# A gated mix of a state-space convolution and a feed-forward network: the block-wise convolution replaced by one 2048-point transform in two TensorE stages

## The chip, the cores and the metric

The kernel runs on one core of a Trainium2 chip. The metric is the time of one execution on the device, in microseconds (us). Times of a kernel are medians of its runs. The five engines named below are TensorE (PE in the profile; PEld is its weight load), VectorE (DVE), ScalarE (ACT), GpSimd (POOL) and SyncE (SP), which here issues nearly all DMA transfers.

A run of one core can be a per cent or two slower than the fastest run of the same kernel. Such runs are marked slow. They are left out of all ratios, but not of the medians quoted; where that matters, the fast runs are given too. (One run of the kernel before took 634.8 us; it too is marked slow.) Chips differ too: the kernel before took 350.6 to 353.1 us (medians) on most of the chips used and 357.3 to 357.7 us on two others, so kernels are compared by their ratio to the kernel before on the same chip wherever a few per cent matter.

## The reference, cut to what matters

```python
# u: [1, 2048, 640] bf16, 128 states per channel, 1728 hidden features
dt = exp(log_dt)[:, None]
logdA = dt * (A_re + 1j * A_im);  dB = dt * (B_re + 1j * B_im)
P = exp(logdA[:, :, None] * l)                       # l = 0..2047
K = einsum("dn,dnl,dn->dl", C_re + 1j * C_im, P, dB).real
y = irfft(rfft(pad(u)) * rfft(pad(K)))[:2048] + u * Dskip     # causal convolution per channel
b = (gelu(u @ w_gate) * (u @ w_up)) @ w_down
g = sigmoid((u * gate_w).sum(-1))
out = g * y + (1 - g) * b
```

Three pieces of work share the core: generating the kernel K (exponentials, sines and a sum over the 128 states), the convolution, and the feed-forward network (FFN).

## The kernel before

Both kernels put all their work into a list of steps, each with its engine, an estimated duration and a priority. A list scheduler in the Python code then fixes the order of instructions on every engine, before anything is built. The order is therefore part of the program: an engine runs its instructions in that order, and a wait at the head of its queue holds up whatever is behind.

K is not evaluated at all 2048 positions. Exponentials and sines are taken on two small grids of positions, for all channels, and a small matmul per channel, summing over the states, combines the two ("the contraction"). The states lie on the 128 partitions, and along the free dimension there are table entries and channels. In the kernel before, four neighbouring channels lie side by side in these tables:

```python
# before: e1[p, channel group k, 4*entry + channel in group]
def quads(ap):
    return ap.rearrange("p (k j) -> p k j", j=4)

def exps1(p, g):
    ...
    nc.scalar.activation(out=e1[:, :, 4 * r:4 * r + 4], in_=quads(aT[:, ds]), func=ACT.Exp,
                         scale=float(sg * (4 + 8 * i)))              # line 420, 128x320
def exps2(p, g):
    ...
    nc.scalar.activation(out=e2[p][:, :, 4 * e:4 * e + 4], in_=quads(aT[:, ds]), func=ACT.Exp,
                         scale=float(X2[e] + CENTRE))                # line 430, 128x320
def sins(k, ph, n, w, dst, keys):                                    # line 466, up to 128x2560
    nc.scalar.activation(out=dst, in_=ph.bitcast(I16)[:, :, :, 0:8 * n:2], func=ACT.Sin, scale=SIN_SCALE)
```

The convolution cuts the 2048 tokens into four blocks. Each block of u and of K is transformed by matmuls with a cosine and sine table, the spectra of all pairs of blocks that matter are multiplied and summed on VectorE (`product`, line 904), and a second set of matmuls transforms back. The inputs are transposed by DMA at the start.

```python
# before: one product of block spectra; n pairs of blocks at once, then selected and summed
def tm(out, a, b, op):
    nc.vector.tensor_tensor(out=out, in0=a, in1=b, op=op)            # line 904
...
ve(..., lambda: tm(x, u[:, ::1 - 2 * q, rev, ds], kb[:, :, 0:n, ds], ALU.mult), ...)
```

## Time and profile before

| | before |
|---|---|
| time, median of 3 runs | 351.87 us (351.23 to 353.12) |
| PE busy | 299.7 us, 84% of the span |
| DVE busy | 297.8 us, 84% |
| ACT busy | 237.2 us, 67% |
| bytes moved by DMA | 25.46 MB |

The head of the profile page of the kernel before: busy time of each engine, then the span in 40 equal slices (8.9 us each), where a digit is the busy share of a slice in tenths. The last row shown is the share of busy time of the 16 DMA engines.

```profile
span 355.9 us, 5682 instructions
...
PE 299.7 (84%) x2182; PEld 175.8 (49%) x2182; DVE 297.8 (84%) x528; ACT 237.2 (67%) x374; POOL 15.7 (4%) x32
...
PE   0048459999999999999785679999999999999885
...
DVE  8999899756368898999893806999999999998962
ACT  6999699999999899999964779999111011100000
...
DMA  6684632003100201102552710052400005003321
```

There are three stages. Until about 43 us PE has little to do. From 60 to 200 us PE and ACT are both nearly full. From 216 us on DVE and PE are full, and from about 250 us ACT is nearly idle. The windows view of the kernel before gives that in numbers (columns: window, its length, then busy time and instructions of PE, PEld, DVE, ACT, POOL, granted clock, DMA share, GB/s):

```profile
60.00:200.00 140.00, 129.56 (x970) 64.83 (x969) 109.76 (x213) 126.78 (x202) 9.00 (x9) 0.99 0.24 66
...
216.00:343.00 127.00, 123.92 (x943) 88.50 (x943) 124.97 (x154) 45.22 (x74) 0.00 (x0) 1.00 0.20 48
```

The groups of instructions of the kernel before (columns: line, engine, operation, output and input with partitions x elements, count, total busy us and mean ns of one instruction, idle time before them; nearly all tiles are cut from one buffer, so most operands read `arena`). The page's group of all sizes of the spectrum products:

```profile
L904 DVE TENSOR_TENSOR arena<-arena 128x640 bf16<-128x640 bf16 (+5 forms) x112 | 106.7, 1011 | 1.5 <-ACT arena L998 0.9
```

From the view of the same kernel that keeps sizes apart:

```profile
L904 DVE TENSOR_TENSOR arena<-arena 128x2560 bf16<-128x2560 bf16 x18 | 26.5, 1489 | 1.1 <-ACT arena L998 0.9
...
L420 ACT ACTIVATE arena<-arena 128x320 bf16<-128x320 f32 x64 | 23.3, 465 | 0.0
...
L466 ACT ACTIVATE arena<-arena 128x2560 bf16<-128x2560 int16 x8 | 18.7, 2343 | 0.8 <-DVE arena L459 0.8
...
L430 ACT ACTIVATE arena<-arena 128x320 bf16<-128x320 f32 x42 | 15.5, 459 | 0.0
```

The spectrum products are a third of all VectorE work. An exponential of 128x320 takes 0.46 us and a sine of 128x2560 takes 2.34 us.

### The profile page before, as it was taken

The page shows a single profiled execution, that of the slowest core. Times are in us where ns is not written, and L with a number is a line of the kernel's source. Part 1 is how long each engine was busy: PE and PEld are TensorE (multiplying, and loading weights), DVE is VectorE, ACT ScalarE, POOL GpSimd, SP SyncE. Part 2 cuts the span into 40 slices and gives each one's busy share as a digit, 9 for nine tenths or more (in the row PEclk, how much of TensorE's full clock was granted, in tenths as well). Part 3 has the DMA queues.
Part 4 walks back from the last instruction along what each step waited for, and adds up shares of the span by engine and source line. Part 5 has one row for each costly group of instructions (what it writes and reads, how often), then busy time and mean ns, then how long its engine had stood idle before and what let it go on. Part 6 is the DMA issues. An engine that isn't in the chain of part 4 may idle for free.

```text
span 355.9 us, 5682 instructions
## 1 busy us (share of the span) xinstructions
PE 299.7 (84%) x2182; PEld 175.8 (49%) x2182; DVE 297.8 (84%) x528; ACT 237.2 (67%) x374; POOL 15.7 (4%) x32
## 2 busy tenths in 40 slices
PE   0048459999999999999785679999999999999885
PEld 0012113444555554444343545666777777767664
DVE  8999899756368898999893806999999999998962
ACT  6999699999999899999964779999111011100000
POOL 6000000000000000000071000000000000000000
PEclk9999988999999999999998989999999999999999
DMA  6684632003100201102552710052400005003321
GB/s 111 181 134 98 163 127 88 20 19 76 37 20 19 58 20 37 40 0 55 187 195 61 276 57 0 2 146 61 103 17 0 20 21 91 20 18 49 100 75 57
DMA packets 53019, 25.46 MB, mean 72 GB/s; under 512 B 46400, under 2 KB 50304, under 8 KB 52608
## 3 DMA queue, kind: packets, MB, share of 16 engines
q1 hardware_dynamic: 52608, 23.79, 26.4%
q0 software_dynamic: 384, 1.31, 1.2%
q8 instruction: 17, 0.28, 0.3%
q14 instruction: 10, 0.08, 0.1%
HBM read 12.83 MB, written 6.03 MB: 53 GB/s over the span
## 4 chain that ended last, share of the span: by engine, by line
DVE 38%; PE 27%; ACT 19%; SPq 10%; issue 4%; DMA 1%; another core or an unknown queue 0%; DVEq 0%; ACTq 0%
DVE arena L904 28%; PE ps L588 10%; PE ps L606 8%; SPq L302 7%; ACT arena L466 5%; ACT arena L529 3%; PE ps L524 3%; DVE arena L883 3%; ACT arena L592 3%; PE ps L1015 2%; ACT arena L430 2%; SPq L307 2%; DVE arena L1024 2%; PE ps L846 2%; ACT arena L660 2%
## 5 line engine op out<-in xcount | busy, mean ns | idle before, releaser
L904 DVE TENSOR_TENSOR arena<-arena 128x640 bf16<-128x640 bf16 (+5 forms) x112 | 106.7, 1011 | 1.5 <-ACT arena L998 0.9
L588 PE MATMUL ps<-arena 128*128 128x512 bf16 x280 | 68.5, 396 | 25.9 <-DMA arena<-in_B_w_gate_dram 21.8
L606 PE MATMUL ps<-arena 128*128 128x512 bf16 x260 | 62.3, 382 | 3.2 <-DVE arena L610 3.0
L994 PE MATMUL ps<-arena 128*128 128x320 bf16 x448 | 62.0, 299 | 0.4 <-ACT arena L872 0.4
L588 PEld LDWEIGHTS <-arena 128*128 128x128 bf16 x280 | 27.9, 101 | 61.7 <-DMA arena<-in_B_w_gate_dram 22.2
L998 ACT ACTIVATE arena<-ps,omg 128x640 bf16<-128x640 f32 x16 | 12.7, 794 | 68.3 <-PE ps L994 61.1
L994 PEld LDWEIGHTS <-arena 128*128 128x128 bf16 x448 | 43.6, 98 | 17.2 <-issue 0.6
L610 DVE TENSOR_TENSOR arena<-ps,arena 128x512 bf16<-128x512 f32 x52 | 34.8, 686 | 17.5 <-PE ps L606 13.7
L466 ACT ACTIVATE arena<-arena 128x2240 bf16<-128x2240 int16 (+1 forms) x20 | 43.3, 2184 | 0.9 <-DVE arena L459 0.8
L606 PEld LDWEIGHTS <-arena 128*128 128x128 bf16 x260 | 24.8, 99 | 33.4 <-issue 7.2
L1015 PE MATMUL ps<-arena 128*128 128x320 bf16 x256 | 37.7, 299 | 2.6 <-DVE arena L1024 1.6
L1015 PEld LDWEIGHTS <-arena 128*128 128x128 bf16 x256 | 24.7, 98 | 12.7 <-issue 3.7
L592 ACT ACTIVATE arena<-ps 128x512 bf16<-128x512 f32 (+1 forms) x56 | 28.5, 615 | 0.3 <-PE ps L588 0.2
L529 ACT CAST arena<-ps 128x420 bf16<-128x420 f32 x32 | 20.3, 674 | 10.9 <-PE ps L524 6.9
L420 ACT ACTIVATE arena<-arena 128x320 bf16<-128x320 f32 x64 | 23.3, 465 | 0.0
L456 DVE SCALAR_TENSOR_TENSOR arena<-arena 128x160 int32<-128x160 f32 x84 | 20.8, 319 | 2.3 <-ACT arena L466 2.2
L846 PE MATMUL ps<-arena 128*128 128x320 bf16 x128 | 20.8, 315 | 1.9 <-ACT arena L850 1.6
L872 ACT CAST arena<-ps 128x640 bf16<-128x640 f32 (+1 forms) x40 | 21.1, 618 | 1.4 <-PE ps L866 0.9
L883 DVE TENSOR_TENSOR arena<-arena 128x640 bf16<-128x640 bf16 (+1 forms) x30 | 11.1, 419 | 12.9 <-ACT arena L872 12.9
L866 PE MATMUL ps<-arena 128*128 128x320 bf16 x144 | 21.1, 299 | 0.8 <-ACT arena L872 0.6
L850 ACT ACTIVATE arena<-ps 128x640 bf16<-128x640 f32 x32 | 20.1, 813 | 1.6 <-PE ps L846 1.6
L655 PE MATMUL ps<-arena 128*128 128x512 bf16 x42 | 13.6, 450 | 8.6 <-ACT arena L660 8.1
(92 smaller groups left out, 310.6 us busy)
## 6 DMA issues: line engine op xcount, KB each, us to landing
out_dram<-arena SPq DMA_DIRECT2D x16, 160.0 KB, 1.8
dFK<-arena SPq DMA_DIRECT2D x9, 256.0 KB, 2.0
arena<-in_B_w_gate_dram SPq DMA_DIRECT2D x13, 160.0 KB, 2.9
arena<-in_B_w_up_dram SPq DMA_DIRECT2D x13, 160.0 KB, 2.7
arena<-in_B_w_down_dram SPq DMA_DIRECT2D x13, 160.0 KB, 2.3
arena<-in_A_u_dram SPq DMA_DIRECT2D x4, 320.0 KB, 4.0
dTAB<-arena SPq DMA_DIRECT2D x1, 1024.0 KB, 4.5
arena<-dTAB SPq DMA_DIRECT2D x1, 1024.0 KB, 5.1
```

Of the source, the lines that this page charges most:

```text
L302: dma(1050, lambda: nc.sync.dma_start_transpose(out=xT[tq][:, kt, :], in_=u2[S * tq:S * tq + S, kt * 128:kt * 128 + 128]), w=[("xT", tq, k ...
L420: nc.scalar.activation(out=e1[:, :, 4 * r:4 * r + 4], in_=quads(aT[:, ds]), func=ACT.Exp, scale=float(sg * (4 + 8 * i)))
L466: ac(actns(2 * n * w), lambda: nc.scalar.activation(out=dst, in_=ph.bitcast(I16)[:, :, :, 0:8 * n:2], func=ACT.Sin, scale=SIN_SCALE), r=[( ...
L529: ac(actns(420), lambda k=k, s=s: nc.scalar.copy(out=kst[:, :, 5 * s:5 * s + 5], in_=ps[:, k, 0:420].rearrange("p (g e) -> p e g", e=84)), ...
L588: nc.tensor.matmul(ps[:, k, :], lhsT=Wg[f % 2][:, kt, :], rhs=xT[tq][:, kt, :], start=(kt == 0), stop=(kt == NKT - 1))
L592: ac(actns(512), lambda: nc.scalar.activation(out=HT[f][0:p, tq, :], in_=ps[0:p, k, :], func=ACT.Gelu_apprx_tanh), r=[("bank", k)], w=[("H ...
L606: nc.tensor.matmul(ps[:, 4 + k, :], lhsT=Wu[f % 2][:, kt, :], rhs=xT[tq][:, kt, :], start=(kt == 0), stop=(kt == NKT - 1))
L610: ve(tt(512, 1) + 60, lambda: nc.vector.tensor_tensor(out=HT[f][:, tq, :], in0=ps[:, 4 + k, :], in1=HT[f][:, tq, :], op=ALU.mult), r=[("ba ...
L846: nc.tensor.matmul(ps[:, k + h, 0:DH], lhsT=tab[:, j, q, fsl(ft)], rhs=src[:, j, h * DH:(h + 1) * DH], start=(j == 0), stop=(j == 1))
L904: nc.vector.tensor_tensor(out=out, in0=a, in1=b, op=op)
L994: nc.tensor.matmul(ps[:, k + h, 0:DH], lhsT=HT[f][:, c, 128 * j:128 * j + 128], rhs=Wd[f][:, h * DH:(h + 1) * DH], start=(f == 0), stop=(f ...
L1015: nc.tensor.matmul(ps[:, k + h, 0:DH], lhsT=tab[:, ft, q, 128 * j:128 * j + 128], rhs=U[ft][:, q, c, h * DH:(h + 1) * DH], start=(ft == 0 ...
```

## The change

The intent is to take the 106.7 us of block products off VectorE and the transposes off the start. One transform of 2048 points replaces the block transforms. It is split into two matmul stages, with a transpose between them that is a write to DRAM scratch and a read in another order. The spectra of u and K are multiplied once, and two more stages, with another scratch transpose, bring the product back. K is written to scratch too and gathered from it in the order of tokens. The FFN runs in two groups of 1024 tokens, so that its VectorE and ACT operations have 1024 columns instead of 512. The host hands u and the parameters over already transposed.

The tables of the kernel generation changed layout with it. The new contraction wants, for one channel, all 20 or 32 table entries adjacent in memory. So the channel became the outer index and the table entry the inner one. The core of the diff, with cuts marked by dots:

```diff
-    def exps1(p, g):                      # e1: groups of four channels side by side
+    def exps1(h, i0, n):                  # cs1 = [128, 2, 320 channels, 32 entries]
...
-                    nc.scalar.activation(out=e1[:, :, 4 * r:4 * r + 4], in_=quads(aT[:, ds]), func=ACT.Exp,
-                                         scale=float(sg * (4 + 8 * i)))
+                    nc.scalar.activation(out=cs1[:, 1, :, s], in_=aT[:, ds], func=ACT.Exp, scale=float(sg * (4 + 8 * i)))
...
+        # cs2 = [128, 2, 320 channels, 20 entries]
+                nc.scalar.activation(out=cs2[:, 1, :, e], in_=aT[:, ds], func=ACT.Exp, scale=float(X2[e] + CENTRE))
...
+        # trig = [128, 2, 320 channels, 4 entries]
+        ac(an(2 * n * W), lambda: nc.scalar.activation(out=t[:, :, :, 0:n].rearrange("p q c j -> p q j c"),
+                                                       in_=ph.bitcast(I16)[:, :, 0:n, 0:2 * W:2], func=ACT.Sin, scale=SIN_SCALE),
...
-                            nc.tensor.matmul(ps[:, k, 84 * g:84 * g + 84], lhsT=cs1[c][:, q, k0 + g, :],
-                                             rhs=cs2[c][:, q, k0 + g, :], start=(q == 0), stop=(q == 1))
+                                nc.tensor.matmul(ps[32 * cg:32 * cg + NE, k + b, 32 * i:32 * i + 32], lhsT=cs2[:, q, c, :],
+                                                 rhs=cs1[:, q, c, :], start=(q == 0), stop=(q == 1))
...
+                evac(256 * nb, p, dst.rearrange("p r (b i) -> p b i r", b=nb), ...)      # PSUM -> kst[128, 32, 80]
...
+        # K to scratch in 20 transfers, gathered to token order in 15
+        for e0, n, r0, rs in ((0, 8, 1, 8), (8, 4, 257, 4), (12, 2, 385, 2), (14, 2, 449, 2), (16, 4, 513, 1)):
+            for cg in range(4): ... dma(n * 5, go, r=KK, w=[(f"dS{h}", e0, cg)], rank=0.5)
...
-    def product(c, ft, hs): ...           # 112 tensor_tensor instructions over the pairs of blocks
+    def chain(h, R):
+            ve(v2(2560), lambda c=c, t=t: nc.vector.tensor_tensor(out=U[c][:], in0=U[c][:], in1=t[:], op=ALU.mult), ...)
+            ve(v2(2560), lambda c=c, t=t: nc.vector.tensor_tensor(out=Us[c][:], in0=Us[c][:], in1=t[:], op=ALU.mult), ...)
...
+            dma(640, lambda s=s, g=g: nc.sync.dma_start(out=dKA[h][8 * g:8 * g + 8].rearrange("i q w -> q i w"), in_=ar[s][:]), ...)
```

Everything that concerns K and the convolution is done for two halves of 320 channels, one after the other.

## The prediction

> **What bounds the kernel now.** Three stages, by the busy time in stretches of 20 us. (1) 0 to 43 us: the sync engine issues DMA transposes at 1.26-1.31 us each (chain of waits); matmul starts late and is 13 of 20 us busy even to 60 us. (2) 60-200 us: ACT (18-20 of 20) and PE share the limit; the chain goes through feed-forward matmuls, sines and gelus. (3) 216-343 us: DVE is full (19-20 of 20) while ACT falls to 3 of 20; the chain is 28% line 904, the block-by-block spectrum products, 106.7 us of DVE (groups by line).
>
> **Costs, with durations from the groups and the chain.** Matmuls stream at 216 ns (512 wide) and 136 ns (320 wide).
> - DVE: products become 16 operations of 128x2560 at 1.49 us = 24 us (-83), the spectrum combining (11), selections and folds (11) go. Added: PSUM copies, about 55 x 0.82 = 45; output mixing 32 x 0.55 = 18 (was 14). Up-multiplications of 128x1024 at about 1.22 = 32 (was 35). The kernel-generation work stays near 100; its 10 magnitude multiplications now broadcast along the innermost dimension and should run unpaired, 1.5 us each (Trainium skill, "Vector Engine (DVE) Microarchitecture Reference", section on the perf-mode triggers; no line of this trace shows it). Sum about 260 (was 298).
> - ACT: sines 18 x 2.34 = 42, exponentials 104 x 0.46 = 48, gelus 29, table loads 23 x 1.28 = 30 (unchanged), about 105 copies x 0.74 = 78. Sum about 243 (was 237), spread evenly.
> - PE: feed-forward 117 + down 61 unchanged; transforms 448 x 136 ns = 61 (was about 96 with its Dskip and FK parts); contraction becomes 1280 32-wide matmuls. The logits show 24.7 ns per pair as floor (80 in 1.98 us), also the skill's figure ("TensorE: Matmul & The Clock Gate", part on the issue floor), so 32-40 us (was about 20). Sum about 275.
> - DMA: 25 MB becomes about 60 MB, mostly through DRAM scratch, half in 640-byte pieces. SP transposes vanish.
>
> **By stages, from the emitted order.** Feed-forward starts at about 10 us instead of 60. Up to the first contraction DVE has 97 us and ACT about 90: ends near 103 us. Then to the second contraction PE, ACT, DVE have each about 75-85 us with dependences: ends near 195 us. After it PE has 117 us (52 of transforms, 30 down, 17 up, 17 contraction), DVE 95, ACT 66, and 30 MB of DMA, estimated 110-135 us because the second stage, spectra and transpose back wait for whole scratch writes. The last write-read-transform-store sequence leaves PE partly idle for about 20 us. Total about 320.
>
> **On the critical path:** about 35-45 us of the start-up, and about 80 us of DVE products; given back: PE's larger contraction, scratch round trips and the drained tail. Not all adds up, because the other engines already hold 240-300 us.
>
> **Predicted: 320 us, range 298 to 342.** Faster by over 2%: 0.84; within 2%: 0.10; slower: 0.06.
>
> **What would show each step.** First feed-forward matmul before 12 us. DVE busy 245-275, ACT 230-255, PE mean of contraction matmuls spaced 25-32 ns. DVE's product group about 24 us. DMA packets moved about 60 MB; its share in the last 120 us above half. In the chain, SP/DMA and PE take over from DVE; sync-queue waits on scratch reads of dKA and dY of several us. Idle of the matmul engine concentrated in the last 30 us.
>
> **What would make it wrong.** The 640-byte scratch traffic may be slower than estimated, or many small kernel gathers (about 35 per half, some 0.4 us each to issue) may hold the queue (toward 345). The clock may drop in the contraction or the idle tail. Or downs and stages overlap so well that PE's total bounds it (toward 300).

## The result and the profile after

The changed kernel is correct and takes 516.12 us (515.19 to 517.49, 4 runs) beside 351.55 us of the kernel before on the same chip. The ratio is 1.468, with a 95% interval of 1.464 to 1.473. A ratio here is the mean time of one kernel's fast runs over the mean of the other's fast runs of the same rounds, so it is not quite the ratio of the medians quoted. The change made the kernel 47% slower. The prediction had said 9% faster.

The same head of the page for the changed kernel (slices of 12.9 us):

```profile
span 514.7 us, 6862 instructions
...
PE 301.8 (59%) x2798; PEld 161.3 (31%) x2798; DVE 254.4 (49%) x331; ACT 402.4 (78%) x302; POOL 4.0 (1%) x15
...
PE   0500685993277743934013698664482879988993
...
DVE  7400366774375635232033365443453458757945
ACT  6999999699996999999999959995562556644410
...
DMA  8800011241024222311001142045085799899767
```

VectorE went from 297.8 to 254.4 us, as intended. PE did not change. The DMA moved 60.66 MB. ACT is the surprise: 402.4 us instead of 237.2, and full from the start to about 350 us.

The groups of the changed kernel by size, with the same columns:

```profile
L614 ACT ACTIVATE arena<-arena 128x2560 bf16<-128x2560 int16 x18 | 105.7, 5958 | 0.1
L625 ACT ACTIVATE arena<-arena 128x320 bf16<-128x320 f32 x64 | 89.8, 1885 | 0.9 <-DVE arena L481 0.9
...
L650 ACT ACTIVATE arena<-arena 128x320 bf16<-128x320 f32 x40 | 56.8, 1897 | 0.0
...
L653 DVE TENSOR_TENSOR arena<-arena 128x1280 bf16<-128x1280 bf16 x10 | 14.9, 1493 | 55.4 <-ACT arena L650 55.4
...
L868 DVE TENSOR_TENSOR arena<-arena 128x2560 bf16<-128x2560 bf16 x8 | 11.9, 1488 | 1.0 <-ACT arena L289 0.9
...
L289 ACT CAST arena<-ps 128x512 bf16<-128x512 f32 x5 | 11.8, 2469 | 12.2 <-DVE arena L293 12.1
```

An exponential of the same 128x320 elements, with the same function and types, takes 1.89 us instead of 0.46. A sine of 2560 elements takes 5.96 us instead of 2.34. (Consecutive instructions overlap: the busy time of the 64 exponentials is 89.8 us, less than 64 x 1.885.) The VectorE groups came out as predicted: 1.49 us for a product of 2560, and 1.49 us for an unpaired one of 1280.

Is this contention with another engine? The changed kernel answers that itself. This is its windows view of one stretch:

```profile
25.00:50.00 25.00, 0.00 (x0) 0.00 (x0) 0.00 (x0) 25.00 (x19) 0.00 (x0) 0.52 0.00 0
```

The timeline of the changed kernel at the start of this stretch (columns: start, duration of the merged entry, engine and line, count):

```profile
21.29 29.68 ACT L625 ACTIVATE arena<-arena 128x320 bf16<-128x320 f32 x21
```

From 25 to 50 us ACT runs exponentials alone. PE, VectorE and GpSimd have no work at all, and the DMA moves nothing. Still 21 exponentials take 29.68 us, one every 1.41 us. In the kernel before, 64 of them make 23.3 us, one every 0.36 us. So the instruction itself became slower, and everything else on the core stands and waits for it. The low granted clock of this stretch (0.52) is TensorE's, which has no work in it. It does not explain ACT: all 64 exponentials of line 625 took 1.61 to 1.93 us, in stretches with a granted clock from 0.50 to 1.00.

What differs in the instruction is its output access pattern. Before, four bf16 results went to adjacent addresses (8 bytes), then a jump. After, each 2-byte result stands alone: the next one is 64 bytes away (line 625), 40 bytes (line 650) or 8 bytes (the sines). The copies out of PSUM (the memory into which TensorE writes its results) after the contraction (line 289, 512 elements, 160 bytes apart) have the same form and take 2.47 us.

### The profile page after: what moved, and what is told of

It reads as the page before. It is cut to its first block, busy times and chain, and to the rows that moved or that the text cites. A ratio compares the mean times of both kernels' runs of the same rounds, so it can differ in the third digit from the quotient of the medians.

```text
span 514.7 us, 6862 instructions
## 1 busy us (share of the span) xinstructions
PE 301.8 (59%) x2798; PEld 161.3 (31%) x2798; DVE 254.4 (49%) x331; ACT 402.4 (78%) x302; POOL 4.0 (1%) x15
## 2 busy tenths in 40 slices
DMA packets 57989, 60.66 MB, mean 118 GB/s; under 512 B 9475, under 2 KB 53318, under 8 KB 57926
## 4 chain that ended last, share of the span: by engine, by line
ACT 26%; PE 12%; DMA 8%; issue 7%; SPq 5%; DVE 4%; ACTq 0%; DVEq 0%
ACT arena L625 9%; ACT arena L614 6%; ACT arena L650 4%; PE ps L578 4%; ACT arena L289 4%; PE ps L876 3%; DMA arena<-dKA 3%; SPq L817 2%; DMA arena<-dU 2%; PE ps L674 1%; SPq L703 1%; PE ps L550 1%; DMA arena<-dY 1%; DVE arena L293 1%; DMA dKA<-arena 1%
## 5 line engine op out<-in xcount | busy, mean ns | idle before, releaser
L289 ACT CAST arena<-ps 128x640 bf16<-128x640 f32 (+2 forms) x110 | 80.9, 808 | 52.0 <-DVE arena L293 12.8
L530 PE MATMUL ps<-arena 128*128 128x512 bf16 x280 | 81.5, 453 | 52.0 <-DMA arena<-in_w_gu_dram 15.9
L614 ACT ACTIVATE arena<-arena 128x2560 bf16<-128x2560 int16 x18 | 105.7, 5958 | 0.1
L625 ACT ACTIVATE arena<-arena 128x320 bf16<-128x320 f32 x64 | 89.8, 1885 | 0.9 <-DVE arena L481 0.9
L293 DVE CAST arena<-ps 128x640 bf16<-128x640 f32 (+2 forms) x62 | 55.9, 923 | 27.0 <-PE ps L847 7.3
L578 PE MATMUL ps<-arena 128*128 128x320 bf16 x448 | 64.3, 303 | 1.4 <-ACT arena L289 1.2
L650 ACT ACTIVATE arena<-arena 128x320 bf16<-128x320 f32 x40 | 56.8, 1897 | 0.0
L744 PE MATMUL ps<-arena 128*128 128x320 bf16 x64 | 15.3, 350 | 67.4 <-DVE arena L295 31.8
L554 DVE TENSOR_TENSOR arena<-ps,arena 128x1024 bf16<-128x1024 f32 x26 | 31.6, 1220 | 28.2 <-PE ps L550 28.2
L653 DVE TENSOR_TENSOR arena<-arena 128x1280 bf16<-128x1280 bf16 x10 | 14.9, 1493 | 55.4 <-ACT arena L650 55.4
L636 DVE TENSOR_TENSOR arena<-arena 128x2560 bf16<-128x2560 bf16 x16 | 23.2, 1490 | 34.9 <-ACT arena L614 19.8
L534 ACT ACTIVATE arena<-ps 128x1024 bf16<-128x1024 f32 (+1 forms) x28 | 27.3, 1024 | 11.3 <-PE ps L530 11.2
L662 DVE TENSOR_TENSOR arena<-arena 128x2560 bf16<-128x2560 bf16 x10 | 14.9, 1493 | 33.8 <-ACT arena L614 33.8
L847 PE MATMUL ps<-arena 128*128 128x320 bf16 x128 | 24.6, 330 | 6.9 <-DMA arena<-dU 3.0
L674 PE MATMUL ps<-arena 128*20 128x32 bf16 x1280 | 12.0, 191 | 17.0 <-issue 14.3
```

What stands on the lines that cost most here:

```text
L289: nc.scalar.copy(out=dst, in_=src(b))
L293: nc.vector.tensor_copy(out=dst, in_=src(b))
L530: nc.tensor.matmul(ps[:, k + j, :], lhsT=Wg[w][:, kt, :], rhs=xT[2 * grp + j][:, kt, :], start=(kt == 0), stop=(kt == NKT - 1))
L534: add({"ACT": an(1024)}, lambda s: nc.scalar.activation(out=HTall[0:p, :, f, :], in_=ps[0:p, plan.bank(g):plan.bank(g) + 2, :], func=ACT.G ...
L554: add({"DVE": v1(1024)}, lambda s: nc.vector.tensor_tensor(out=HTall[:, :, f, :], in0=ps[:, plan.bank(u):plan.bank(u) + 2, :], in1=HTall[: ...
L578: nc.tensor.matmul(ps[:, k + h, 0:W], lhsT=HTq[q][:, f, 128 * j:128 * j + 128], rhs=Wd[f][:, W * h:W * h + W], start=(f == 0), stop=(f == ...
```

## The experiments

The first theory (call it W) is that the lone 2-byte writes with a step cost the time, and that their excess, 173 us of ACT time, was nearly all on the critical path. The 173 us are the three groups above less the same work at the old durations, as runs 2 and 3 later measured it: (89.8 - 23.2) + (56.8 - 14.6) + (105.7 - 41.6). Rivals are that the scratch traffic (60 MB) or stages that wait for each other cost it and ACT only looks busy, or that the work of ACT differs in some way other than layout.

### 1. Only the sines' walk turned

The sine instruction visits its elements in another order: it now writes contiguously and takes its step, 1280 bytes, on the reading side.

```diff
-  activation(out=t[:, :, :, 0:n].rearrange("p q c j -> p q j c"), in_=ph.bitcast(I16)[:, :, 0:n, 0:2 * W:2], ...)
+  activation(out=t[:, :, :, 0:n], in_=ph.bitcast(I16)[:, :, 0:n, 0:2 * W:2].rearrange("p q j c -> p q c j"), ...)
```

> Only the order in which the 18 sine activations walk their elements is turned: reads step over the rows of the phase buffer, writes are contiguous. Theory W (ACT is slowed by writes whose neighbouring 2-byte elements are 8 to 64 bytes apart, and ACT then bounds the first 370 us): one sine falls from 5.96 us to about 2.3 us, ACT busy from 402 to about 340 us, time from 516 to about 450-465 us. Rival D (the DRAM scratch traffic and the drained tail cost the time): the time stays above 490 us even if the sines are faster. Rival C (ACT is slowed by other engines or DMA using the memory at the same time): a sine stays near 6 us. If strided reads cost as much as strided writes, a sine stays near 6 us too.

Measured: 495.6 us, ratio 1.411 (1.401 to 1.421), correct. The sine group in this run:

```profile
L614 ACT ACTIVATE arena<-arena 128x2560 bf16<-128x2560 int16 x18 | 84.1, 4706 | 0.1
```

This is a miss in size. The time fell by 20.5 us with the 21.6 us that the group lost, so ACT time was time of the kernel. But the instruction came down only from 5.96 to 4.71 us, not to 2.3. A step on the reading side costs as well, though less. Here, moving the step from one side of the instruction to the other did not remove the cost.

### 2. Groups of four channels, on both sides

The tables of the changed kernel get the old grouping: four adjacent channels, then the table entries, then the groups. Reads and writes are then both in runs of at least four. The contraction's matmuls pay instead: they read their 20 and 32 elements with a step of four.

```diff
-    cs1 = at(O_CS1, [128, 2, W, 32], BF16, "cs1")
+    cs1 = at(O_CS1, [128, 2, W // 4, 32, 4], BF16, "cs1")
...   (the same for cs2, trig, ph)
-    nc.scalar.activation(out=cs1[:, 1, :, s], in_=aT[:, ds], func=ACT.Exp, ...)
+    nc.scalar.activation(out=cs1[:, 1, :, s, :], in_=quads(aT[:, ds]), func=ACT.Exp, ...)
...
-    lhsT=cs2[:, q, c, :], rhs=cs1[:, q, c, :]
+    lhsT=cs2[:, q, c // 4, :, c % 4], rhs=cs1[:, q, c // 4, :, c % 4]
```

> The factor tiles, phases and sines are laid out in groups of four channels, so that exponentials, sines and the magnitude multiplication write runs of at least 4 elements; TensorE then reads both operands of the contraction with a step of 4 elements. Theory W: exponentials take about 0.46 us (start to start 0.36) instead of 1.89 (1.40), sines 2.3 us, ACT busy about 220-235 us, time 315-345 us, near the blind prediction of 320. Rival D: above 450 us. Separate risk: the contraction, 29.6 ns per matmul now, may rise with the stepped reads; at twice that it adds 38 us to PE.

Measured: 348.4 us, ratio 0.990 (0.985 to 0.995), correct; 3 us above the 315 to 345 us expected. ACT is busy for 231.3 us. The three groups, by size:

```profile
L617 ACT ACTIVATE arena<-arena 128x2560 bf16<-128x2560 int16 x18 | 41.5, 2339 | 1.6 <-DVE arena L613 1.5
...
L628 ACT ACTIVATE arena<-arena 128x320 bf16<-128x320 f32 x64 | 23.2, 455 | 0.9 <-DVE arena L481 0.9
...
L655 ACT ACTIVATE arena<-arena 128x320 bf16<-128x320 f32 x40 | 14.6, 459 | 0.0
```

The durations are back at those of the kernel before, and 168 us of the 516 are gone, with all bytes, stages and scratch transfers in place. This settles the main cause. The 171 us that ACT lost became 168 us of kernel time.

### 3. The copies after the contraction turned too

On top of run 2, the copies out of PSUM write along the adjacent channels, and the step goes to the PSUM side.

```diff
-   evac(256 * nb, p, dst.rearrange("p r (b i) -> p b i r", b=nb), ... "p b (i s) -> p b i s" ...)
+   evac(256 * nb, p, dst.rearrange("p r (b i) -> p b r i", b=nb), ... "p b (i s) -> p b s i" ...)
```

> The run with groups of four, and the copies out of the contraction walk their elements the other way round, so that they write 16 neighbours instead of elements 160 bytes apart. Theory W: the 512-element copies fall from about 2.5 us to about 0.7 us on both ACT and DVE, about 18 us of busy time over both engines; a few of them lie between contraction and scratch write, so the time falls by 3-10 us against the run with groups of four. If a stepped read from PSUM costs as much as a stepped write, no change.

Measured: 345.35 us, ratio 0.976 (0.970 to 0.982), correct. Two of its four runs are marked slow, the profiled one among them; the fast ones took 342.04 and 343.41 us, 5 us less on average than run 2. In a later set on the same chip the same kernel took 344.62 us, ratio 0.981, with all four runs and the profile fast (run 16). This is called the mended kernel below. Two groups of it, by size:

```profile
L658 DVE TENSOR_TENSOR arena<-arena 128x1280 bf16<-128x1280 bf16 x10 | 8.0, 814 | 1.6 <-ACT arena L655 1.6
...
L289 ACT CAST arena<-ps 128x512 bf16<-128x512 f32 x5 | 2.9, 610 | 19.5 <-DVE arena L293 19.5
```

A copy (line 289) went from 2.47 to 0.61 us. Here the read with a step of 32 fp32 in PSUM costs little, unlike the read of run 1. The other line is a side effect of the grouping. The magnitude multiplication, 1.49 us in the changed kernel (line 653), takes 0.81 us, because its broadcast is no longer along the innermost dimension. The Trainium skill, "Vector Engine (DVE) Microarchitecture Reference", section 5.1 on performance modes, asks for a step of one in the innermost dimension of every 2-byte operand before two results per cycle are made. The two durations agree with that.

### 4. The kernel before, with its exponentials walked in another order

The opposite test. The kernel before writes exactly the same results to the same addresses, but its 106 exponentials go through them channel by channel instead of in fours.

```diff
-   nc.scalar.activation(out=e1[:, :, 4 * r:4 * r + 4], in_=quads(aT[:, ds]), func=ACT.Exp, ...)
+   nc.scalar.activation(out=e1[:, :, 4 * r:4 * r + 4].rearrange("p k j -> p j k"),
+                        in_=quads(aT[:, ds]).rearrange("p k j -> p j k"), func=ACT.Exp, ...)
...   (the same for e2)
```

> The kernel before, with its 106 exponentials walking the same elements in another order: neighbours in the walk are then 168 or 256 bytes apart in the output and 16 bytes in the input. Same values, same bytes, nothing else moved. Theory W: one exponential goes from 0.46 us to about 1.9 us (start to start 0.36 to 1.40), ACT busy from 237 to about 345 us, time from 352 to 430-460 us. Rivals C and D, which look for the cause in the new kernel's traffic: no change above 10 us.

Measured: 468.82 us, ratio 1.335 (1.327 to 1.343), correct; somewhat more than the 430 to 460 us expected. The two groups, by size:

```profile
L420 ACT ACTIVATE arena<-arena 128x320 bf16<-128x320 f32 x64 | 91.9, 1929 | 0.0
L431 ACT ACTIVATE arena<-arena 128x320 bf16<-128x320 f32 x42 | 59.4, 1870 | 0.0
```

The order in which one instruction walks through the same addresses makes it four times slower and this kernel 118 us slower than its runs beside it. ACT's busy time rose by 112 us. The effect needs nothing else of the change. (These instructions also read with a step of 16 bytes. Run 9 shows that such a read alone gives 0.75 us, so it does not explain 1.9 us.)

### 5. Groups of two

Two accounts of the write cost remained open: either every 16-byte line touched costs a fixed 4.4 ns, whatever is written to it, or it is the write of less than 4 bytes that costs. Groups of two channels touch twice the lines of groups of four, but every write has 4 adjacent bytes. The edit is run 3 with `W // 2` and `j=2` in place of `W // 4` and `j=4`.

```diff
-    cs1 = at(O_CS1, [128, 2, W // 4, 32, 4], BF16, "cs1")
+    cs1 = at(O_CS1, [128, 2, W // 2, 32, 2], BF16, "cs1")
...
-        return ap.rearrange("p (k j) -> p k j", j=4)
+        return ap.rearrange("p (k j) -> p k j", j=2)
```

> The mended kernel (groups of four channels, contraction copies turned), with groups of two instead of four: the exponentials write runs of 2 elements (4 bytes), 80 or 128 bytes apart. Theory L (a write costs about 4.4 ns for each 16-byte line that it enters, so 1.40 us for 320 lone elements, 4.7 ns for the sines' two elements a line): 160 lines take 0.70 us start to start, exponentials 73 us of ACT in all instead of 38, time 345 to about 350-365 us. Rival T (two neighbours are enough for full speed): start to start stays 0.36 us, time unchanged. Rival S (any break in the walk costs the same as none adjacent): back to 1.4 us.

Measured: 347.16 us, ratio 0.988 (0.984 to 0.993), correct. Its exponentials:

```profile
L628 ACT ACTIVATE arena<-arena 128x320 bf16<-128x320 f32 x64 | 23.4, 463 | 0.9 <-DVE arena L481 0.9
L655 ACT ACTIVATE arena<-arena 128x320 bf16<-128x320 f32 x40 | 15.8, 514 | 0.0
```

Two adjacent results are enough (0.46 and 0.51 us; 0.37 us from start to start in the first group). At 4.4 ns for each of the 160 lines it would have been 0.70 us. So writes of 4 bytes do not pay that price. A smaller cost per line is not excluded (run 9).

### 6. A wider contraction

This concerns the remaining gap to 320 us. In the changed kernel the contraction's matmuls come in bursts. The timeline of PE in the changed kernel, with the idle time before each entry in brackets:

```profile
357.61 1.23 PE L674 MATMUL ps<-arena 128*20 128x32 bf16 x128 [4.57 <-issue]
361.34 1.21 PE L674 MATMUL ps<-arena 128*20 128x32 bf16 x128 [2.50 <-issue]
```

128 pairs of weight load and matmul take 1.2 us, or 9.6 ns a pair, and then PE mostly stands for 2.5 us. The period is 3.73 us, or 29 ns a pair. The run asks what the pauses are: it makes every matmul 64 columns wide. (It computes surplus columns and overwrites some results.)

```diff
-   nc.tensor.matmul(ps[32 * cg:32 * cg + NE, k + b, 32 * i:32 * i + 32], ..., rhs=cs1[:, q, c // 4, :, c % 4], ...)
+   nc.tensor.matmul(ps[..., 32 * min(i, 14):32 * min(i, 14) + 64], ..., rhs=cs1[:, q, min(c // 4, 78):min(c // 4, 78) + 2, :, c % 4], ...)
```

> The mended kernel with the contraction's matmuls 64 columns wide instead of 32 (wrong result on purpose; the same count, the same instruction words). Now 128 pairs are issued in 1.24 us and then nothing for 2.5 us, 29.2 ns per pair. Theory F (PE waits for its instructions to be fetched, 256 at a time): the bursts get longer, the period of 3.73 us per 128 pairs stays, the two contractions stay near 18.7 us each. Rival A (PE's array or a floor per matmul, with trace records displaced): the period grows by 128 x 13 ns = 1.7 us or more.

Measured: 350.61 us (one run, its state unknown). PE's timeline in this run:

```profile
109.08 2.13 PE L680 MATMUL ps<-arena 128*20 128x64 bf16 x127
112.58 2.15 PE L680 MATMUL ps<-arena 128*20 128x64 bf16 x128 [1.38 <-issue]
```

The bursts grew by 0.9 us, the pauses shrank by 1.1, and the period stayed (3.5 us). So the pause is not a rest that PE needs after its work. PE waits for something that comes every 256 instructions, at a pace that does not depend on the matmul's width. The Trainium skill, "Runtime: NRT & Kernel Launch", section "Instruction fetch mechanics", says that an engine's instructions are fetched in blocks of 16 KiB, 256 instructions, and that crossing a block costs a DMA step that is "mostly hidden". The number 256 agrees. The "mostly hidden" does not for pairs this small: 2.5 of every 3.73 us are pause.

No run changed the fetch itself, but the kept traces show it. The page of the changed kernel has, among its DMA queues (packets, MB, share of the 16 engines):

```profile
q8 instruction: 22, 0.36, 0.3%
```

These are 22 packets of 16 KiB, for 5596 weight loads and matmuls (21.9 blocks of 256); the kernel before has 17, for 4364. In the second contraction one such packet lands before each burst after the first: at 359.94 us for the burst at 361.34, at 363.82 us for the next. In the second contraction of the changed kernel, of run 3 and of this run, these bursts start 1.25 to 1.6 us after their packet has landed. A packet takes 0.9 to 1.4 us, and the next one mostly starts 1.0 to 1.2 us after the burst, whether its matmuls have 32 or 64 columns. These three times make up the period. So PE is waiting for its instructions.

### 7. First weights and tokens loaded first

```diff
-   wl: rank=2                x_load: rank=1
+   wl: rank=0.2 for the first loads    x_load: rank=0.3 for the first two, 1.6 for the others
```

> The mended kernel with the first gate and up weights and the first half of x loaded ahead of the rest (ranks of loads changed; the list scheduler then orders the rest anew). The first feed-forward matmul now runs at 18 us and the next waits for weights until 26.5 us. If that late start matters: steady matmul from about 11 us, time 345 to 333-340 us. If the first 105 us are bound by kernel generation on ACT and DVE: no change beyond 3 us.

Measured: 353.78 us, ratio 1.007 (1.003 to 1.010), correct, which is 2% worse than run 5 on the same chip and 3% worse than the mended kernel. PE was busy for 8.2 us of the first 20 instead of 3.6, but for 14.3 instead of 18.4 in the next 20. The 333 to 340 us of the first theory were missed. This fits a first stage bound by kernel generation, in which FFN work done earlier is only missing later. But the scheduler planned all engines anew here too, so the cause of the loss is not isolated.

### 8. Fewer bytes: the swap copies

The spectra need a copy of U with its two halves of partitions exchanged. An eighth of it is copied here. Its output is wrong, which doesn't matter for the time.

```diff
-   dma_start(out=Us[c][64 * s:64 * s + 64], in_=U[c][64 - 64 * s:128 - 64 * s])
+   dma_start(out=Us[c][64 * s:64 * s + 64, 0:1], in_=U[c][64 - 64 * s:128 - 64 * s, 0:1])
```

> The mended kernel, with the 16 copies that swap halves of the spectrum cut to one eighth of their bytes (wrong result on purpose): 4.6 MB less of about 30 MB in the last 105 us. If transfers bound that stage (share of the 16 engines 0.74 to 1.05 there, about 280 GB/s): 12-17 us less. If PE or the order of dependences does: under 5 us.

Measured: 336.42 us (2 runs), ratio 0.958 (0.950 to 0.966). The 4.6 MB left out are worth 6 to 8 us by the mended kernel's ratios on another chip, or 11 us against run 5 on the same chip. That is between what the two theories expected.

### 9. The access patterns measured by themselves

The mended kernel, with a bench at its end: copies of 320 elements per partition, eight of each form, on ACT and VectorE.

```python
for _ in range(8): nc.scalar.copy(out=ob[:, 0:320:1], in_=f4[:, 0:320:1])       # L930: adjacent bf16 writes
for _ in range(8): nc.scalar.copy(out=ob[:, 0:640:2], in_=f4[:, 0:320:1])       # L932: 4 bytes apart
...  # L934: 8 bytes, L936: 16, L938: 32, L940: 64; L942: runs of two, 128 bytes apart
...  # L946: lone fp32 writes 16 bytes apart; L952: fp32 reads 64 bytes apart; L970: as L938, but on VectorE
```

> The mended kernel with a bench appended after its last instruction: 16 groups of 8 copies of 320 elements on ACT, then the same on DVE, which differ only in the step of the output or the input; only the durations of the groups count, not the time. From the runs so far: on ACT a contiguous write is about 0.45 us; lone 2-byte writes 8 bytes apart about 0.9-1.0 us (the sines' 2.33 ns per element), 32 or 64 bytes apart about 1.9 us; runs of two 0.46-0.51 us wherever they lie; what 4 and 16 bytes apart cost is open. If the cost is of a write smaller than 4 bytes, lone 4-byte outputs 16 and 64 bytes apart stay near 0.45 us; if it is of a write that has no neighbour, they rise to 1.9 us like the 2-byte ones. Inputs: 4-byte inputs 16 bytes apart no dearer (the kernel before with turned walks showed none), further apart perhaps up to 2x. DVE: from the contraction's copies (2.57 us for 512 elements 160 bytes apart), 1.6 us for lone 2-byte writes far apart, 0.5 us contiguous.

The kernel is correct; its time (499.5 us) says nothing. Groups of this run by line:

```profile
L936 ACT CAST arena<-arena 128x320 bf16<-128x320 f32 x8 | 12.9, 1607 | 0.3
...
L934 ACT CAST arena<-arena 128x320 bf16<-128x320 f32 x8 | 7.2, 906 | 0.3
...
L970 DVE CAST arena<-arena 128x320 bf16<-128x320 f32 x8 | 6.7, 835 | 0.3
...
L946 ACT COPY arena<-arena 128x320 f32<-128x320 f32 x8 | 6.0, 753 | 0.3
...
L952 ACT CAST arena<-arena 128x320 bf16<-128x320 f32 x8 | 5.8, 724 | 0.3
...
L932 ACT CAST arena<-arena 128x320 bf16<-128x320 f32 x8 | 4.4, 552 | 0.3
...
L942 ACT CAST arena<-arena 128x320 bf16<-128x320 f32 x8 | 3.7, 464 | 0.3
L930 ACT CAST arena<-arena 128x320 bf16<-128x320 f32 x8 | 3.7, 458 | 0.2
```

On ACT, adjacent writes take 458 ns; lone bf16 writes take 552 ns at a step of 4 bytes, 906 at 8, and 1526 to 1607 at 16, 32 and 64. Runs of two are free even 128 bytes apart. A lone 4-byte write costs half as much as a lone 2-byte one (726 to 753 ns in all), and a read with a step of 16 bytes or more costs about as much as that (724 to 751 ns). VectorE shows the same shape: 327 ns adjacent, 522 at 8 bytes, 835 to 874 at 16 and more, 329 to 332 for runs of two. Two of these were not expected: reads with a step were thought to be free at 16 bytes, and a lone 4-byte write was to cost either nothing extra or as much as a lone 2-byte one.

The numbers follow one sum, an estimate from this bench. The time stops rising at a step of 16 bytes, so count the 16-byte lines that an instruction enters. Lone bf16 writes enter 80, 160 and 320 of them at steps of 4, 8 and 16 bytes, and 552, 906 and 1607 ns are 200 ns plus 4.4 ns a line. The lone 4-byte writes, the stepped reads and the runs of two fit 1.7 ns a line, which for the 160 lines of the runs of two is no more than the adjacent copy takes anyway. The kernel's own instructions fit as well: a sine of 1280 lines would take 5.8 us (5.96 measured), a copy of 512 lines 2.5 us (2.47), and the sine of run 1, with 2560 stepped reads, 4.5 us (4.71). The exponentials, which overlap, start 1.40 us apart, which is 320 lines without the fixed part. Why a line entered with 2 bytes costs more than one entered with 4 is not shown. That each narrow write must first read what is there does not fit by itself: at a step of 4 bytes four such writes share a line, and the instruction is only a fifth slower.

### 10 to 12. The second half's K transfers on another queue

In the mended kernel PE stands still for 11 us in the last stage. The timeline of run 3 (its profile is of a slow run; in run 16, a fast one, the same pause is 10.88 us):

```profile
216.64 3.16 PE L838 MATMUL ps<-arena 128*128 128x320 bf16 x18 [0.28 <-ACT arena L289]
230.77 6.33 PE L550 MATMUL ps<-arena 128*128 128x512 bf16 x20 [10.97 <-DMA arena<-in_w_gu_dram]
```

The load of feed-forward weights that PE waits for is queued on the sync engine behind the 20 small writes of the second half's K to scratch. These runs issue the 35 K transfers of that half elsewhere: from ACT's queue (10), from GpSimd's (11), and from ACT's with the scheduler told 29 ns for a contraction pair (12).

```diff
+    def dmaq(h, kb, fn, ...):
+        q = nc.scalar if h == 1 else nc.sync           # run 11: nc.gpsimd
...
-            p = pe(128 * nb * 16, go, ...)
+            p = pe(128 * nb * 29, go, ...)             # run 12 only
```

> The mended kernel, with the 35 transfers that carry the second half of K to scratch and gather it back issued from ACT instead of SP. SP is busy issuing without a pause from 203 to 249 us there (42 us of issues), and the chain of waits follows it. If that queue bounds the start of the last stage: its first K transform comes 10-20 us earlier and the time falls from 345 to 328-338 us. If the scratch bandwidth or PE bounds it: under 4 us.

> As the run with the ACT queue, but from POOL, which has nothing else to do in that stage; its descriptors are made in software (mirror gathers of the kernel before took 1.1 us each to issue). 35 issues at 1.1 us or more are about 40 us: not better than SP unless ACT's copies are what the ACT variant delays. 335-350 us.

> The run with the ACT queue, with the list scheduler told that the contraction takes 29 ns per pair of instructions (measured) instead of 8; only the order of instructions changes. If the order chosen for a contraction too short is costing time: 3-8 us less than with the ACT queue alone; else the same within 3 us either way.

Measured, all correct, on a chip where the kernel before took 357.7 us: 355.35 us, ratio 0.995 (0.990 to 1.001); 360.27 us, ratio 1.005 (1.000 to 1.010), its profiled run slow; 353.65 us, ratio 0.992 (0.987 to 0.997). All three are worse than the mended kernel's 0.976 and 0.981, but it was not run on this chip, so by how much is not shown. The gain of 7 to 17 us hoped for from run 10 did not come, run 11 lies above the 335 to 350 us expected, and run 12 is within 3 us of run 10. In run 10 the sync queue had only four transfers to issue from 225 to 248 us, but ACT stood for 16.5 us up to 231 us, until K writes that it now issued itself had landed, and PE for 8.5 us behind it. These runs changed the order of all engines as well, because the scheduler plans anew.

### 13 and 14. Fewer bytes in the last stages; few transfers for K

Run 13 reads an eighth of the second-stage and last-stage inputs and of the swaps. Run 14 carries K with 5 transfers a half instead of 35. Their outputs are wrong, which doesn't matter for the times.

```diff
# run 13
-   dma_start(out=bi[s][:], in_=v[:, 8 * c:8 * c + 8, :])
+   dma_start(out=bi[s][:, 0:1], in_=v[:, 8 * c:8 * c + 1, :])
-   dma_start(out=ar[s][:], in_=dY[h][8 * g:8 * g + 8]...)
+   dma_start(out=ar[s][:, 0:1], in_=dY[h][8 * g:8 * g + 1]...)
# run 14
-   for e0, n, r0, rs in ((0, 8, 1, 8), (8, 4, 257, 4), (12, 2, 385, 2), (14, 2, 449, 2), (16, 4, 513, 1)):
+   for e0, n, r0, rs in ((0, 8, 1, 8),):
...   (and one gather instead of 15)
```

> The mended kernel with the second-stage loads, the loads of the last stage and the half swaps cut to one eighth of their bytes (wrong result on purpose; every transfer, dependence and instruction is still there): about 18 MB less of about 36 MB from 185 us on. If bytes bound the last stage: 25-40 us less than the mended kernel. If the order of dependences and issues does: under 12 us.

> The mended kernel with K carried by 5 transfers per half instead of 35 (wrong result on purpose; the gather moves the same bytes in one transfer). If the number of issues on the SP queue is what delays the last stage: 12-25 us less. If only the latency of scratch and the order matter, as the ACT queue run suggests: under 6 us.

Measured: 333.61 us, ratio 0.948 (0.941 to 0.956), and 353.58 us, ratio 1.002 (0.995 to 1.009). Cutting most of the reads of the last stages saves only 11 us, under the 12 us of the second theory, so the scratch bytes are not the main part of what is missing. In run 14 the 11 us pause is gone and the up matmuls end at 245 instead of 256 us, but the end of the kernel has new pauses: PE waits 8.63 us at 338 us for the read of the last scratch (dY). The run is 9 us slower than run 16, which neither theory expected. Again the plan had changed.

### 15 and 16. Half a contraction; the mended kernel again

```diff
-                        for q in range(2):
+                        for q in range(1):             # run 15; wrong on purpose
```

> The mended kernel with half of the contraction's matmuls (the sine term left out, wrong result on purpose): 640 pairs fewer, 18-19 us of PE time by the period of 3.73 us per 128 pairs. If the contraction lies wholly on the critical path, 15-19 us less; if other work of the stage fills in, 5-10 us.

> The mended kernel once more (groups of four, contraction copies turned, nothing else), for comparison on the chip of these runs: 0.97 to 0.98 of the kernel before.

Measured: 328.27 us, ratio 0.929 (0.921 to 0.936), its profiled run slow; and 344.62 us, ratio 0.981 (0.976 to 0.987). Half the contraction is worth 16 us by the medians and 18 us by the fast runs alone, so nearly all of its 37 us (1280 pairs at 29 ns) lie on the critical path. (Run 15 passed the comparison although half of the sum was missing, and so did run 6. The wrong K of run 14 failed it. So a pass is weak evidence about K.)

### 17. Weight loads first, by priority

The weight loads get a higher priority (a lower rank) than the K writes, on the same queue.

```diff
-   dma(160, lambda: nc.sync.dma_start(out=t[:], in_=w_gu...), w=[nm], rank=2)
+   dma(160, lambda: nc.sync.dma_start(out=t[:], in_=w_gu...), w=[nm], rank=0.4 if nw[False] + nw[True] > 4 else 2)
```

> The mended kernel with one priority changed: from the fifth weight tile on, the loads of the feed-forward weights go ahead of the scratch writes of the second half's K on the sync engine's queue (in the mended kernel's profile TensorE is idle for 10.97 us at 219.8 us, and the profile names the weight load as what ended it). Theory Q (head of line: those 11 us are lost time): the idle stretch goes and the kernel takes 334 to 340 us, a ratio to the kernel before of about 0.95 to 0.965 (mended: 0.976 and 0.981). Theory T (the tail is bound by its own chain of scratch round trips and whatever is gained before it is given back there, as in the runs with other issuing queues): the idle stretch goes, the ratio stays at 0.975 to 1.0, and the idle time turns up in the last 40 us.

Measured: 387.76 us, ratio 1.100 (1.091 to 1.108), correct, and 12% worse than the mended kernel, which neither theory expected. The windows view of this run:

```profile
260.00:280.00 20.00, 20.00 (x150) 14.41 (x148) 4.42 (x5) 0.00 (x0) 0.00 (x0) 1.00 0.09 28
```

PE's timeline of this run around that window:

```profile
257.56 26.78 PE L578 MATMUL ps<-arena 128*128 128x320 bf16 x196
284.18 0.98 PE L838 MATMUL ps<-arena 128*128 128x320 bf16 x6
```

The wait for weights became shorter, but did not go: PE still stands 7.41 us for a load, up to 228.85 us. With most weights early, the FFN was ready early, and the scheduler placed 196 down matmuls (line 578) in one piece ahead of six matmuls of the transform's first stage (line 838). The sync queue then waited 26.9 us for the copy of that transform. The DMA engines fell to a share of 0.09, and ACT had nothing to do. PE was full and the kernel lost time: it did filler work while the chain of scratch round trips stood still.

### 18. The same two loads moved, all other orders kept

After the plan is made, two weight loads move forward on the sync queue. The traces of runs 16 and 18 show the same order of instructions on PE, VectorE and ACT.

```diff
     plan.run()
+    o = plan.order          # move the weight loads of the last K writes ahead, to right behind what they depend on
+    for s in [s for s in o[first:last + 12] if s["aset"] == "w"]:
+        o.remove(s)
+        o.insert(max([first] + [k + 1 for k, d in enumerate(o) if d["i"] in s["deps"]]), s)
```

> The mended kernel with the order of every engine's work kept as it is, and two loads of feed-forward weights moved forward on the sync engine's queue, in between the scratch writes of the second half's K (they stood behind all of them). In the run before this one the same aim, reached by a priority, changed the order of TensorE too: 196 down matmuls in one piece ran ahead of a first-stage transform, the DMA engines were idle meanwhile, and the kernel took 388 us. Theory Q (the idle 10.97 us of TensorE at 219.8 us is lost time): with the order fixed the idle stretch shrinks to under 3 us and the ratio to the kernel before falls by 0.015 to 0.03, to 0.945 to 0.965 (338 to 340 us). Theory T (the chain of scratch round trips bounds the stage, the filler work only moves): the stretch shrinks, the ratio stays at 0.97 to 0.985.

Measured: 343.98 us, ratio 0.962 (0.958 to 0.966), correct. The kernel before took 357.29 us on this chip, and the mended kernel was not run there. By its ratio alone theory Q would have won. But the ratio can't be set beside 0.976 and 0.981 without care: in absolute time the run equals the mended kernel (344.62 and 345.35). The traces decide more. PE's timeline of this run:

```profile
234.11 0.69 PE L838 MATMUL ps<-arena 128*128 128x320 bf16 x2 [9.95 <-DVE arena L554]
...
252.39 2.32 PE L550 MATMUL ps<-arena 128*128 128x512 bf16 x10
```

The second of these instructions in run 16, the mended kernel:

```profile
252.38 2.32 PE L550 MATMUL ps<-arena 128*128 128x512 bf16 x10
```

ACT's timeline of this run in the same stretch:

```profile
230.58 4.86 ACT L788 ACTIVATE arena<-arena,mQ 128x1024 bf16<-128x1024 bf16 x2 [10.89 <-DMA dS<-arena]
```

The weights arrived, 20 matmuls ran at once, and then PE stood for 9.95 us after all, now for VectorE. ACT and VectorE stood too: the next instruction on each fills a table that reuses the memory of K's staging tile, so it waits until the last of the 20 small scratch writes has read that tile. Behind that instruction, in order, stands the multiplication that PE needs. In run 16, on another chip, the matmul that starts at 252.39 us here starts at 252.38 us, and both spans are 342.4 us. From the first transform after the contraction to that matmul it is 52.9 us there and 52.6 us here. So the stretch was not lost to the weight load. By the traces it was lost to the wait for the small writes, and taking away the first wait only uncovered the second; no run took this second wait away with the order kept. (The table instruction itself, line 788, writes lone bf16 results 8 bytes apart, and its two executions on ACT take 4.86 us: the cost of run 9 once more.)

## Why the prediction was wrong

**The step that failed** is in the prediction's ACT sum: "sines 18 x 2.34 = 42, exponentials 104 x 0.46 = 48". The counts were right. The durations were read from the kernel before, from instructions of the same function and size but with another output layout, and carried over. Measured: sines 18 at 5.96 us, 106 us busy; exponentials 64 + 40 at 1.89 us, 147 us busy. ACT came to 402 us instead of "243". With it went the path by stages: the first contraction, to begin when the work before it "ends near 103 us", began at 186 us, and the second at 352 us, where the prediction had it over "near 195". This is nearly the whole miss: with the old grouping alone (run 2) 168 of the 196 us are gone, and the kernel takes 348 us, with run 3 about 345. The same cause lies behind the smaller surprise in the contraction's copies (2.5 us instead of 0.6). The diff showed the new output pattern in plain sight. It was looked at for VectorE, where the rule about an innermost broadcast was applied, and not for ACT. The list of what could make the prediction wrong had DMA traffic, issue time and clock, and no entry for a duration that depends on the layout.

**What held:**
- VectorE: about 260 us predicted, 254.4 measured. Products "24 us": 16 of 1.49 us, 23.8 us. Unpaired magnitude multiplications "1.5 us each": 1.49. Up-multiplications "1.22": 1.22.
- PE: "about 275" predicted, 273.0 in the mended kernel. (In the changed kernel it was 301.8, at a mean granted clock of 0.81.)
- DMA "about 60 MB": 60.66 MB.
- The contraction: "25-32 ns" a pair, 29 ns measured; 37 us in sum. The mean was right and the reason was not. The prediction read the 24.7 ns of the logits as a floor of issue, with the Trainium skill, "TensorE: Matmul & The Clock Gate", section "Back-to-back issue gap", which gives about 25 ns for up to 64 columns. Here pairs ran at 9.6 ns within a burst of 128, and a pause for the next 256 instructions made the mean. That the two came to the same was luck. (The contraction's matmuls go in turn to four groups of 32 output partitions, the logits' do not; in the trace of the changed kernel a set of four starts every 33 ns or so.)

**What was off in the direction of hope, once ACT is mended** (345 against 320 us, just outside the range):
- "First feed-forward matmul before 12 us": 15.9 us, since the load was queued behind the parameters. Run 7, which loaded it earlier, gained nothing.
- The stages up to the second contraction were near the prediction: it begins at about 185 us in the mended kernel and ends at 202 us, against "ends near 195".
- The last stage was "estimated 110-135 us" after the second contraction and is 143 us (202 to 345). The transfers of K were put at "some 0.4 us each to issue". The 20 writes took 0.83 us each on the sync queue, 16.7 us, as the sum of their issue entries from 203 to 228 us. That list of small transfers holds up ACT, VectorE and PE for some 10 us (run 18). The scratch bytes that runs 8 and 13 left out are worth 6 to 11 us. These overlap, and they are not a complete account.

**What stays open.** No run brought the mended kernel below 342 us with a full result. Each attempt that moved the small transfers by the scheduler changed the plan of all engines and ended slower than the mended kernel, by its ratio (runs 10, 11, 12 and 14), or much slower (run 17). Whether the pause goes, and the time with it, when the table no longer reuses the memory of the staging tile is not tried. The difference between the ratio of run 18 and that of the mended kernel can be the chip's and is not claimed as a gain.

The mended kernel, with or without run 18's order, is 2 to 4% faster than the kernel before on the same chips (0.976, 0.981, 0.962; the first two are clear of 1, but not of a mark of 2%) and is the best correct version found. So the idea of the change was sound by a small margin, and its layout cost it 168 us.

## What to carry to other kernels

A duration read from a trace belongs to a size, a type and an access pattern: before carrying it over, write down for each instruction which bytes its innermost loop touches, on the reading and on the writing side, and take lone 2-byte results on ACT as twice as dear 8 bytes apart and three to four times from 16 bytes on, until measured. Where a matmul wants another order than the engines that fill its operands, let the matmul have the step: groups of two or four kept ACT at full pace here, and the contraction's bursts of 128 pairs stayed at 1.25 us. And when filler work is moved in an ordered queue, look at what the next instruction in each queue waits for, since removing the first wait may only uncover the second.

## What the Trainium skill lacked or had wrong

- "SBUF — State Buffer", the note on 16-byte cachelines under "Door 1: The DMA port swizzle", says that bf16 can be strided for free up to 8 elements, with two hits a line for full bandwidth ("Advanced Engine Details and Errata", section "SBUF Cachelines", has the same two hits). For writes of bf16 it does not hold: 320 elements took 458 ns adjacent, 552 at a step of two elements, 906 at four (two hits a line) and 1607 at eight.
- Neither page tells reads from writes or 2-byte from 4-byte writes. At steps of 16 to 64 bytes on ACT, lone 2-byte writes took 1526 to 1607 ns, lone 4-byte writes 726 to 753, reads 724 to 751; runs of two bf16, even 128 bytes apart, took 464. By the estimate of run 9 a line entered costs ACT 4.4 ns with a lone 2-byte write and 1.7 ns otherwise.
- Apart from these notes on cachelines, no page read says that an ACT instruction's time depends on its output pattern. Here it went from 0.46 to 1.89 us for 128x320 and from 2.34 to 5.96 us for 128x2560.
- "Runtime: NRT & Kernel Launch", section "Instruction fetch mechanics", calls the cost of crossing a 16 KiB block "mostly hidden". In a stream of 32-column weight load and matmul pairs PE mostly paused 2.5 us after 256 instructions, two thirds of the time.
- "TensorE: Matmul & The Clock Gate", section "Back-to-back issue gap": about 25 ns as floor for up to 64 columns. The logits agree (24.7 ns). Within bursts the contraction's 32-column pairs ran at 9.6 ns (1.23 us for 128) and the 64-column ones at 16.8 ns (2.15 us for 128), but they go in turn to four groups of output partitions, so this does not show the floor to be wrong.
